# Loading q and k separately in another order, and a new instruction order, in a fused chunk-attention and token-mixing kernel

## Chip, core and metric

The kernel runs on one core of one Trainium2 chip. The metric is the device time of one execution in microseconds (us). The engines are TensorE (PE; its weight loads are listed apart as PEld), VectorE (DVE), ScalarE (ACT), GpSimd (POOL) and SyncE (SP). POOL and SP issue DMAs, each through its own queue; ACT can issue them too.

## What is computed

Inputs q, k, v are [8, 8, 576, 64] (batch, head, token, feature) in float32. Attention is within chunks of 64 tokens; its output, heads side by side, is the input x [8, 576, 512] of a mixing layer over the tokens:

```python
scores = scale * q_c @ k_c.T            # each chunk of 64 tokens, each head
attn   = exp(scores - max) / (sum + 1e-9)
x      = attn @ v_c                     # -> [B, S, 512]
wq, wk = x @ w_q, x @ w_k               # 512 -> 64
mixed  = (1/8 * wq @ wk.T) @ x          # over all 576 tokens of a batch
out    = relu(mixed) @ w_out            # float32 [8, 576, 512]
```

There is no softmax in the mixing, so the kernel computes `wq @ (wk.T @ x)`: G = wk.T x is a 64 x 512 matrix per batch.

## The kernel before

**Units.** The work is cut into 20 units, the list `pairs`. For each two batches there are five: two stretches of 256 tokens of the first batch, the last 64 tokens of both batches together (a "rest", units 2, 7, 12, 17), and two stretches of the second batch. Unit 19 is the last.

**Steps of a unit.** `turns` turns q and k with TensorE into PSUM (`tq`; two steps, q then k, in a whole unit, one in a rest) and evicts them to `qbd` (q in two halves) and `kt`. `attention` makes the scores (`S`, L407), the row maximum on DVE (`mx`, L420), the difference on DVE (`sub`, L431), exp on ACT (L441), turns the result (`E`, L453), evicts it (`et`), multiplies with v (`V`, L484; v carries a column of ones, which gives the sum), and then DVE adds 1e-9, takes the reciprocal and scales (`den`, `rec`, `x`). `project` turns x (`xT`, L536), evicts (`xt`), multiplies with the two small weights (`pj`, L553) and turns the wk part (`wkT`, `wkn`). `mixing` sums G over a batch (L607), evicts it (`g16`), multiplies with wq (`mix`, L647), applies relu on the way out (`rm`), multiplies with w_out (`out`, L696), evicts (`osb`) and stores. Evictions and casts can go to ACT or DVE; most of them stand under one helper, L308.

**The order.** Nothing is scheduled when the kernel is built. The string `ORDER` lists every step by its number with the engine behind it (p PE, a ACT, v DVE, s a store) and the PSUM banks that it takes; each engine runs its own steps in that order. An entry such as `i7.512` is a filler: a product of ones into bank 7, 512 columns wide, whose result is not used (L740). The string was made by a planner outside the kernel.

**The loads.** `LOADS` lists the loads in the order of GpSimd's queue: in the old kernel `q5` stands for q and k of unit 5, one DMA each (two each in a rest), `v5` for its v (two DMAs). Only q and k of unit 0 come by SP's queue, as float32 (`wide_in`), and are cast to f16 by ACT or DVE; the DMAs of GpSimd's queue cast on the way. `load_more` issues the list until it meets a v whose place in `v_all` is still held by an earlier unit; it goes on when that unit's V steps have been put in the order. The tiles of q and k lie in a pool of seven (`HOMES["qk"]`). The queue has eight completion semaphores, so that a load also waits for the landing of the eighth before it; the same holds for the stores.

**The stores.** A store is issued by SP. A tiny DMA (`held`, L268) that reads the last element of unit 4's v stands ahead of all stores in SP's queue.

Of the kernel before, what the change touches and what calls it, by code (L numbers as in the profile page):

```python
# [34 lines left out]


NQB, NG, NV = 3, 3, 8

HELD = 4
LATE = {("qk", 1, 0): 2.5, ("qk", 1, 1): 2.0}  # L40

HOMES = {
# [21 lines left out]
    "rm2": 3,  # L64
    "rm1": 2,
}
LOADS = "q1 v0 q2 v1 wqk v2 q3 q4 v3 q5 wo v4 q6 v5 q7 v6 q8 v7 q9 v8 q10 v9 q11 v10 q12 v11 q13 v12 q14 v13 q15 v14 q16 v15 q17 v16 q18 v17 q19 v18 v19"

ORDER = """
0a 1v i7.256 i6.256 i5.256 i7.256 i6.256 i5.256 i7.256 i6.256 i5.256 i7.256 i6.256 i5.256 i7.256 i6.256 i5.256
i7.256 i6.256 i5.512 i7.256 i6.256 7p0 3a 2a 9a 8v i7.512 i6.512 i5.512 i7.512 i6.512 i5.512 i7.512 i6.256
i5.256 10p1 11a i7.256 26p5 28a 4a 27a i7.256 12p0 29p4 13v 30a 14v 15a i7.512 i6.512 i3.512 i7.512 i6.256 31p4
32v i7.512 i6.512 i3.512 i7.256 53p0 55v 33v i7.512 i6.256 16p1 54a 56a 17a 34a i7.512 i6.512 i3.512 i7.512
i6.256 18p0 22p6 i5.256 57p4 i3.512 35p5 36a 23v 19v 20v 58v 24v 59v 21v 37p2 41p4 38v 60a 39v 42v 25v 61p0
88p1 62a 63p6 89a 90a 45p0 40v 64v 43v 65v 44v 91p2 66v i3.256 47p1 92a 67p3 93p6 107p2 i5.512 110p4 109a 108a
68a 46a 48v 6v 94v 5v 95v 111v i3.256 69p5 49p3 70v 71p2 72v 112p4 113v 96a 50a 97p6 51p7 98a 52v 153p3 156p6
73p7.2 103p0 154a 155a 157a 75a 74a 114v 99p4 104v 105v 100v 101v 106v 102v 115a 158p2 76p6 159v 77a 78p0 116p4  # L80
126p5 79a 117v 160v 118p6 122p0 84p4 172p2 175p3 123v 124v 119v 125v 173v 174v 120v 85v 121v 161a 127a 162p5
176a 163a 177p2 168p4 164p0 128p6 129a 199p6 130p7 178v 165v 166v 179v 169v 167v 82p2 131v 170v 200a 202a 201a
180a 203p6 132p7 204v 83a 171v 181p3 234p2 133a 182a 134p7.0 183p4 237p3 236a 136a 235a 135v 205v 184v 185v
186v 238a 137p0 239p2 139p6 206a 138a 207p4 86p5 208a 140a 253p4 240v 241v 256p0 209p6 187p2 255a 254a 242a
143p1 191p4 192a 257v 188v 189v 190v 210v 211v 258p2 212v 259v 145p0 146a 260v 193p4 243p6 194a 244a 87a 87s
299p0 302p4 249p6 245p2 300a 301a 144v 213p5 214a 195p1 196a 261a 250v 251v 246v 303v 252v 247v 248v 215p0
304p4 80p6 149p2 216a 217p7 197p0 150a 198a 305v 218v 318p1 306v 219p0.7 321p2 221v 322v 220a 319a 320a 222p4
272p7 223v 224p2 273a 323p0 262p7 324v 225a 263a 307a 147p4 226p5 345p7 325v 268p0 264p2 148a 148s 81v 81s 269v
265v 270v 266v 271v 227v 267v 308p4 230p6 346a 348a 347a 326a 309a 231a 349p7 380p0 310p4 314p2 383p6 350v 351v
315v 311v 312v 316v 382a 381a 352a 274p1 327p7 328a 151p0 275a 384v 385p6 313v 317v 386v 276p1 353p2 277a 152a  # L90
152s 354a 387v 228p3 229v 229s 337p1 278p0 338a 279a 333p4 329p6 334v 330v 335v 331v 332v 336v 399p2 280p3.0
402p1 355p6 282v 356v 357v 358v 401a 281a 400a 388a 232p3 339p0 340a 283p4 284v 359p2 285p6 341p0 403a 360a
342a 233a 233s 286v 404p4 361p2 389p1 343p0 295p6 362a 363p2 344a 364a 390a 296a 405v 406v 445p3 365p2.0 448p1
366v 367a 447a 395p6 449v 289p0 141p2 370p4 293p1 142a 142s 407a 294a 290a 396v 397v 398v 446v 371v 450p2 451v
408p6 368p4 297p7 409a 369a 298a 298s 467p6 464p0 466a 465a 452v 468v 414p2 410p4 391p6 392v 411v 415v 393v
394v 412v 416v 413v 417v 291p1 376p0 469p6 470v 374p4 453a 454p5 375a 471v 455a 420p2 418p4 421a 419a 377a
491p5 456p2 460p6 287p4 472a 493v 494v 457v 492v 461v 462v 463v 495p5 458v 496v 497v 459v 422p0 378p6 423a 288a
288s 424p0 473p7 425a 529p4 426p0.5 474v 498a 379a 379s 530a 475p6 428v 479p2 427a 476v 480v 526p4 292a 292s
477v 481v 478v 545p0 527a 528a 482v 429p6 499p1 430v 431p2 531p4 500a 432a 485p1 532v 548p6 501p2 502v 439p7
547a 549a 546a 503v 504v 533v 483p6 440a 484a 486a 534a 505p0 550p2 372p7 441p4 487p1 535p6 373a 373s 442a 551v  # L100
506v 552v 437p7 507p0 536a 553a 537p2 488v 508v 541p4 538v 509p6 489p0 542v 539v 554p1 510a 543v 540v 544v 490a
555a 511p0.6 560p2 556p4 561v 557v 562v 558v 559v 563v 438a 438s 512a 513a 564p7 516p0 435p6 514p4 566p2 443p3
515v 565a 517a 567a 568p2 433p7 569a 444a 444s 570p2 436a 434a 434s 571v 522p4 572p6.5 524p7 525a 574v 573v
# [6 lines left out]
def kernel(  # L110
# [10 lines left out]
    nc = tc.nc  # L121
# [120 lines left out]
    for e in LOADS.split():  # L242
        u = int(e[1:]) if e[1:].isdigit() else None
        rest = u is not None and pairs[u][1] is None
        if e == "wqk":
            landing("w", 1.7)
            loads.append((load_w, [], None))
        elif e == "wo":
            landing("wo", 3.3)
            loads.append((load_wo, [], None))  # L250
        elif e[0] == "q":
            for t in range(2):
                landing(("qk", u, t), 0.94 if rest else wide)
            loads.append((load_qk, [u], None))
        else:
            landing(("v", u), halves if rest else 2 * halves)
            loads.append((load_v, [u], next((w for w in heir_v if heir_v[w] == u), None)))


    made_v, held, opened = {None: 2}, [], []  # L260

    def load_more():
        while loads and made_v.get(loads[0][2], 0) == 2:
            load, args, _ = loads.pop(0)
            load(*args)

            if load is load_v and args == [HELD]:
                nc.sync.dma_start(const.tile([1, 2], F16, name="held")[:], v_all[0:1, slot[HELD] + 1, H - 1, D - 2 : D])  # L268
# [4 lines left out]
    def store(to, of):  # L273
        if opened:
            nc.sync.dma_start(to, of)
        else:
            held.append((to, of))

    load_more()

# [56 lines left out]
    def turns(u):  # L337
# [40 lines left out]
        for t in range(2):  # L378
            bk = Banks(1)

            def pe(t=t, bk=bk):
                tp = in_banks(bk, 512, F16)[:, 0].rearrange("p (j x r g) -> p j x r g", j=HP, x=4, r=R)
                for j in range(HP):
                    for r in range(R):
                        for o in range(2):
                            of = qk[u][:, t, 2 * j + o, r * D : r * D + D]
                            nc.tensor.transpose(tp[half(o), j, :, r, :], of, ident[:])  # L387

            n1 = add("tq", {"PE": 8 * 0.056}, pe, ready[t] if u == 0 else [landed(("qk", u, t))], form=TALL, takes=[bk], size=16)
            if u in heir:  # L390
# [4 lines left out]
    def attention(u, made):  # L395
# [73 lines left out]
        for fours in ([0], [1]) if m is not None else ([0, 1],):  # L469
# [6 lines left out]
            def pe_v(fours=fours, xp=xp):  # L476
# [14 lines left out]
                made_v[u] = made_v.get(u, 0) + 1  # L491
                load_more()

            den, rec = [], []

# [187 lines left out]
    def outs(u, at_tok, deps):  # L683
# [4 lines left out]
        for i in range(ni):  # L688

            wide = DM // 2 if (b, m, i) == (B - 1, NPB - 1, 1) else DM  # L690
            for at in range(0, DM, wide):
# [17 lines left out]
                def send(i=i, s=s):  # L709
                    t0 = 0 if m is None else 2 * P * m  # L710
                    if m is None:
                        for c in range(2):
                            store(out[b + c, S - C : S, :], osb[0][half(c), i, :])
                    elif turned(u, 1):
                        store(out[b, t0 + i * P : t0 + i * P + P, s], osb[0][:, i, s])
                    else:
                        rows = out[b, t0 : t0 + 2 * P, :].rearrange("(x p) d -> p x d", p=C)
                        for c in range(2):
                            store(rows[:, 1:3] if c else rows[:, 0:4:3], osb[0][half(c)])
# [14 lines left out]

    steps = [n for n in nodes if n.cost]
    for e in ORDER.split():
        what, eng, *at = re.split(r"([ipavs])", e, maxsplit=1)
# [5 lines left out]
        if eng == "s":  # L743
            n.send()
            continue
        for bk, i in zip(n.takes, at):
            bk.at = i
# [29 lines left out]
```

## Time and profile before

| what | value |
|---|---|
| median of 3 runs | 138.56 us (138.06 to 140.58) |
| the profiled execution's own time | 138.08 us |
| its span | 136.3 us, 4971 instructions |
| granted TensorE clock, mean | 0.995 |
| DMA traffic | 29.62 MB read from HBM, 9.44 MB written |
| fillers (L740) | 52, of them 30 of 256 and 22 of 512 columns |
| loads on GpSimd's queue | first issued at 1.43 us, last landing at 104.9 us |
| first store issued, last landing | 55.7 us, 134.97 us |

The span is what the profiler recorded of one execution; the time around it is some 1.8 us longer. A wait in the profile is put down to what came last by the trace. TensorE's matmuls overlap, and the ends that the profile shows are modelled, so that a full PE in a stretch does not say that nothing more fits in.

### The profile page before, as it was taken

The page shows a single profiled execution, that of the slowest core. Times are in us where ns is not written, and L with a number is a line of the kernel's source. Part 1 is how long each engine was busy: PE and PEld are TensorE (multiplying, and loading weights), DVE is VectorE, ACT ScalarE, POOL GpSimd, SP SyncE. Part 2 cuts the span into 40 slices and gives each one's busy share as a digit, 9 for nine tenths or more (in the row PEclk, how much of TensorE's full clock was granted, in tenths as well). Part 3 has the DMA queues.
Part 4 walks back from the last instruction along what each step waited for, and adds up shares of the span by engine and source line. Part 5 has one row for each costly group of instructions (what it writes and reads, how often), then busy time and mean ns, then how long its engine had stood idle before and what let it go on. Part 6 is the DMA issues. An engine that isn't in the chain of part 4 may idle for free.

```text
span 136.3 us, 4971 instructions
## 1 busy us (share of the span) xinstructions
PE 122.2 (90%) x2124; PEld 82.8 (61%) x2124; DVE 109.6 (80%) x210; ACT 100.0 (73%) x175; POOL 74.3 (55%) x96
## 2 busy tenths in 40 slices
PE   6999978897859999999999999999999998999910
PEld 4566556575546667776676867566677766544500
DVE  5429898899899799999999999989989998535220
ACT  6186674789738997969996878795888998568500
POOL 7969998745789896469992642679410000000000
PEclk9999999999999999999999999999999999999997
DMA  3999999999999999999999999999999614628883
GB/s 83 273 169 155 131 171 170 182 190 175 156 156 170 172 176 170 166 236 153 173 207 292 175 279 185 241 207 220 200 164 300 227 37 121 154 64 206 280 248 124
DMA packets 86249, 25.08 MB, mean 184 GB/s; under 512 B 78932, under 2 KB 81748, under 8 KB 86228
## 3 DMA queue, kind: packets, MB, share of 16 engines
q0 software_dynamic: 78752, 14.29, 130.1%
q1 hardware_dynamic: 7476, 10.49, 25.3%
q8 instruction: 16, 0.26, 0.7%
q14 instruction: 5, 0.04, 0.1%
HBM read 29.62 MB, written 9.44 MB: 287 GB/s over the span
## 4 chain that ended last, share of the span: by engine, by line
PE 61%; DVE 20%; ACT 10%; issue 3%; DVEq 1%; ACTq 0%
PE ps L696 21%; PE ps L387 7%; DVE mx L420 6%; PE ps L740 5%; DVE sh L431 5%; PE ps L536 5%; PE ps L484 5%; PE ps L647 4%; PE ps L407 4%; PE ps L453 4%; PE ps L553 3%; ACT es L441 3%; PE ps L607 2%; DVE xs L512 2%; ACT rm L669 2%
## 5 line engine op out<-in xcount | busy, mean ns | idle before, releaser
L696 PE MATMUL ps<-wo,rm 128*128 128x512 f16 (+1 forms) x148 | 35.7, 374 | 0.0
L229 POOL DMA_DIRECT2D v_all<-in_v_dram x33 | 29.0, 896 | 11.5 <-DMA qk<-in_k_dram 4.4
L512 DVE TENSOR_TENSOR xs<-ps,rec 128x512 f16<-128x512 f32 x36 | 23.9, 684 | 0.4
L420 DVE TENSOR_REDUCE mx<-ps 128x16 f32<-128x1024 f32 (+1 forms) x20 | 22.2, 1110 | 1.5 <-PE ps L407 1.3
L441 ACT ACTIVATE es<-sh 128x1024 f16<-128x1024 f32 (+1 forms) x20 | 19.5, 975 | 2.7 <-DVE sh L431 2.5
L308 ACT COPY qbd<-ps 64x512 f32<-64x512 f32 (+1 forms) x33 | 18.1, 548 | 4.1 <-PE ps L387 2.4
L387 PE MATMUL ps<-ident,qk 128*64 128x128 f16 x512 | 19.6, 221 | 1.2 <-DMA qk<-in_k_dram 1.0
L696 PEld LDWEIGHTS <-rm 128*128 128x128 f16 x148 | 13.2, 98 | 12.2 <-issue 0.2
L308 ACT COPY osb<-ps 128x512 f32<-128x512 f32 (+1 forms) x28 | 15.8, 586 | 6.5 <-PE ps L696 6.4
L431 DVE TENSOR_TENSOR sh<-ps,mx 128x1024 f32<-128x1024 f32 x16 | 19.5, 1221 | 0.4
L387 PEld LDWEIGHTS <-qk 128*64 128x64 f16 x512 | 15.7, 109 | 4.7 <-issue 1.5
L215 POOL DMA_DIRECT2D qk<-in_k_dram x15 | 13.5, 902 | 3.4 <-DMA v_all<-in_v_dram 1.7
L215 POOL DMA_DIRECT2D qk<-in_q_dram x15 | 13.8, 918 | 1.8 <-DMA qk<-in_k_dram 1.4
L669 ACT ACTIVATE rm<-ps 128x1024 f16<-128x1024 f32 (+1 forms) x13 | 14.1, 1098 | 0.5 <-PE ps L569 0.3
L407 PEld LDWEIGHTS <-qbd 128*128 128x128 f16 x288 | 10.7, 98 | 4.5 <-DVE qbd L308 1.2
L740 PE MATMUL ps<-ones 128*128 128x256 f16 (+1 forms) x52 | 12.2, 372 | 1.2 <-DVE ones L157 1.2
L407 PE MATMUL ps<-kt,qbd 128*128 128x64 f16 x288 | 11.9, 193 | 1.1 <-DVE qbd L308 0.5
L308 ACT COPY xt<-ps 128x512 f32<-128x512 f32 (+1 forms) x18 | 9.6, 554 | 3.3 <-PE ps L536 3.0
L484 PE MATMUL ps<-v_all,et 64*64 64x65 f16 x576 | 9.8, 195 | 2.3 <-ACT et L308 0.7
L453 PE MATMUL ps<-ident,es 128*128 128x128 f16 x144 | 11.4, 220 | 0.2 <-DVE den L498 0.2
L308 ACT COPY et<-ps 128x512 f32<-128x512 f32 (+1 forms) x18 | 9.7, 541 | 2.0 <-PE ps L453 1.9
L536 PE MATMUL ps<-ident,xs 128*128 128x128 f16 x144 | 11.0, 220 | 0.1
(57 smaller groups left out, 172.5 us busy)
## 6 DMA issues: line engine op xcount, KB each, us to landing
out_dram<-osb SPq DMA_DIRECT2D x31, 256.0 KB, 5.2
v_all<-in_v_dram POOLq DMA_DIRECT2D x31, 128.0 KB, 7.7
qk<-in_q_dram POOLq DMA_DIRECT2D x15, 256.0 KB, 7.4
qk<-in_k_dram POOLq DMA_DIRECT2D x15, 256.0 KB, 8.0
out_dram<-osb SPq DMA_DIRECT2D x10, 128.0 KB, 2.8
v_all<-in_v_dram POOLq DMA_DIRECT2D x10, 64.0 KB, 6.3
osb<-in_q_dram SPq DMA_DIRECT2D x1, 512.0 KB, 4.2
osb<-in_k_dram SPq DMA_DIRECT2D x1, 512.0 KB, 5.5
```

Source lines behind the costliest of these rows:

```text
L215: nc.gpsimd.dma_start(qk[u][:, t], rows)
L229: nc.gpsimd.dma_start(v_all[on, slot[u] + i, :, 0:D], v[b, :, of, :].rearrange("h p d -> p h d"))
L308: (nc.vector.tensor_copy if eng == "DVE" else nc.scalar.copy)(to, of)
L387: nc.tensor.transpose(tp[half(o), j, :, r, :], of, ident[:])
L407: nc.tensor.matmul(sp[:, i, j, c ^ turned(u, i), :], lhsT=st["qb", u][:, j, x].rearrange("p o s -> p (o s)"), rhs=st["kt", u][:, j, x * C ...
L420: nc.vector.tensor_reduce(mx[:], scores(), axis=AX.X, op=ALU.max)
L431: nc.vector.tensor_tensor(out=sh[:].rearrange("p x (g r) -> p x r g", r=R), in0=in_banks(bs, 512).rearrange("p i (x r g) -> p (i x) r g", ...
L441: nc.scalar.activation(es[:].rearrange("p x s -> p (x s)"), st["sh", u][:].rearrange("p x s -> p (x s)"), AF.Exp, scale=scale_attn,)
L512: nc.vector.tensor_tensor(out=to, in0=xp()[:, :, :, 0:D], in1=by, op=ALU.mult)
L536: nc.tensor.transpose(tx[:, f, i, :], xs[u][:, i, 2 * f : 2 * f + 2, :], ident[:])
L696: nc.tensor.matmul(in_banks(bo, wide)[:, 0], lhsT=st["rm", key][:, f, at_tok + i * P : at_tok + i * P + P], rhs=wo[:, f, s], start=(f == 0 ...
L740: nc.tensor.matmul(ps[:, at[0], 0 : at[1]], lhsT=ones[:, 0:P], rhs=ones[:, 0 : at[1]], start=True, stop=True)
```

## The change

`LOADS` has entries `Q5` and `K5` of their own, and another sequence. `load_qk` takes the parts that it is to load and makes the tile at the first of them. A load of q or k, like one of v, is now issued when both steps that read its place's former holder have been put in the order. The tiny DMA ahead of the stores and the list of held stores are gone. A store names its queue: `s` is SP's, `t` ScalarE's. `ORDER` is another one over the same steps, with 48 fillers; one store has the `t`.

```diff
-LOADS = "q1 v0 q2 v1 wqk v2 q3 q4 v3 q5 wo v4 q6 v5 q7 v6 q8 v7 q9 v8 q10 v9 q11 v10 q12 v11 q13 ...
+LOADS = "Q1 K1 Q3 K3 Q2 K2 v0 Q4 K4 v1 v2 Q5 K5 wqk v3 Q6 K6 v4 Q7 K7 wo v5 Q8 v6 K8 Q9 v7 K9 Q10 K10 Q11 Q12 K11 K12 v8 Q13 K13 v9 v10 v11 ...
 ORDER = """
-0a 1v i7.256 i6.256 i5.256 ...
-i7.256 i6.256 i5.512 i7.256 i6.256 7p0 3a 2a 9a 8v i7.512 i6.512 i5.512 i7.512 i6.512 i5.512 i7.512 i6.256
-i5.256 10p1 11a i7.256 26p5 28a 4a 27a i7.256 12p0 29p4 13v 30a 14v 15a ...
+1v 0a i7.256 i6.256 i5.256 ...
+i7.256 i6.256 i5.512 i7.256 i6.256 7p0 8v 3a 2v 6a 9a i7.512 i6.512 i5.512 i7.512 i6.512 i5.512 i7.256 10p1 11a
+i7.512 i6.512 i5.512 i7.256 12p0 26p7 13v 29p6 88p5 14v 28a 27a 30a i4.512 i3.512 i2.512 i4.512 91p7 15a i6.256
+31p0 92v 32v 89a ...
 ...
-523v 523s 577p2 575p0 578a 518p7 520p6 576v 519a 521a 521s 589p0 581p7 583p6 585p2 579p3 590a 584a 584s 586a
-586s 587p2 591p6 580v 592v 588v 582a 582s 592s 588s
+523a 523s 578a 520p0 576v 518p1 521v 581p6 583p0 519a 519s 584a 584s 579p1 580v 582a 582s 589p2 587p0 585p6
+590a 591p1 586a 592v 588a 588s 592s 586t
 """
-    def load_qk(u):
+    def load_qk(u, ts=(0, 1)):
         b, m = pairs[u]
-        if m is None:
+        if u in qk:
+            pass
+        elif m is None:
             qk[u] = const.tile([P, 2, H, D], F16, name=f"qk{u}")
 ...
-        for t, x in enumerate((q, k)):
+        for t in ts:
+            x = (q, k)[t]
 ...
-    def load_more():
-        while loads and made_v.get(loads[0][2], 0) == 2:
+    def load_more(key=None):
+        if key is not None:
+            made_of[key] = made_of.get(key, 0) + 1
+        while loads and (loads[0][2][1] is None or made_of.get(loads[0][2], 0) == 2):
             load, args, _ = loads.pop(0)
             load(*args)
-
-            if load is load_v and args == [HELD]:
-                nc.sync.dma_start(const.tile([1, 2], F16, name="held")[:], v_all[0:1, slot[HELD] + 1, H - 1, D - 2 : D])
-                opened.append(True)
-                for to, of in held:
-                    nc.sync.dma_start(to, of)
 ...
-            store(out[b, t0 + i * P : t0 + i * P + P, s], osb[0][:, i, s])
+            by.dma_start(out[b, t0 + i * P : t0 + i * P + P, s], osb[0][:, i, s])
 ...
-            n.send()
+            n.send(nc.sync if eng == "s" else nc.scalar)
```

In the last two rows of `ORDER`, 588 and 586 are the two half-width evictions of unit 19's last 128 tokens, 584 the full one before them, 580 and 582 those of unit 18, 592 that of the last rest; 589 and 590 are the last rest's mix and rm, 591 its out.

More of the change, by code (lines that the diff above doesn't have):

```diff
@@ L66 @@
 }
-LOADS = "q1 v0 q2 v1 wqk v2 q3 q4 v3 q5 wo v4 q6 v5 q7 v6 q8 v7 q9 v8 q10 v9 q11 v10 q12 v11 q13 v12 q14 v13 q15 v14 q16 v15 q17 v16 q18 v17 q19 v18 v19"
+LOADS = "Q1 K1 Q3 K3 Q2 K2 v0 Q4 K4 v1 v2 Q5 K5 wqk v3 Q6 K6 v4 Q7 K7 wo v5 Q8 v6 K8 Q9 v7 K9 Q10 K10 Q11 Q12 K11 K12 v8 Q13 K13 v9 v10 v11 Q14 K14 v12 Q15 K15 Q16 v13 K16 v14 Q17 K17 v15 Q18 v16 K18 v17 Q19 K19 v18 v19 "
 ORDER = """
-0a 1v i7.256 i6.256 i5.256 i7.256 i6.256 i5.256 i7.256 i6.256 i5.256 i7.256 i6.256 i5.256 i7.256 i6.256 i5.256
@@ new lines @@
+78p4 161a 123v 119v 124v 125v 120v 76p2 77a 121v 126p0 199p1 79v 177p6 200a 128p2 127a 178v 162p3 202a 129a
+163a 201a 130p2 179v 131a 180a 203p3 84p1 204v 82p2 205v 85a 168p6 206a 132p3 181p1 169v 83v 164p4 170v 182a
+234p2 165v 133v 166v 171v 134p3.1 236a 167v 235a 183p6 136a 187p4 135a 191p2 188v 184v 189v 207p3 190v 185v
+139p0 137p4 140a 192v 186v 138v 237p2 253p6 208a 238a 209p0 255a 193p7 210v 239p4 211v 194a 212v 256p2 254a
+240v 213p7 195p6 214a 257v 149p0 241v 215p7 145p2 216a 196a 217p7 150v 242a 258p4 218v 302p6 259v 299p7 303a
@@ new lines @@
+318p3 300a 146v 86p6 301a 260v 320a 197p2 304p0 198a 243p7 319a 305v 87a 87s 244a 143p2 345p3 306v 219p6.4 348a
+144a 321p7 347v 221a 220a 249p0 245p4 261a 346v 246v 250v 80p6 251v 247v 248v 322a 349p3 81a 81s 323p4 222p6
+350v 223a 252v 262p2 351v 224p0 263a 324v 147p3 225a 272p6 325v 380p2 273a 383p7 352a 382v 268p4 264p0 265v
+151p6 381a 266v 269v 270v 267v 384a 230p2 326a 271v 385p0 274p7 353p4 231v 307a 386v 327p2 275a 308p5 328a
+276p7 354v 309a 387v 148a 148s 314p4 277a 226p2 315v 316v 152a 152s 317v 278p7 310p0 279a 333p4 227a 311v 399p6
@@ new lines @@
+334v 312v 335v 313v 280p7.3 402p2 336v 281v 329p0 403a 355p4 330v 228p7 337p2 401a 331v 356v 332v 357v 282a
+338a 400a 358v 339p3 283p0 285p4 340v 284v 359p2 286a 341p6 232p3 360v 388a 342v 295p4 404p0 296a 343p6 361p2
+405v 141p4 344a 362a 363p2 448p6 142a 142s 364v 406v 365p2.5 229a 229s 464p4 449a 233v 233s 445p7 367a 366a
+407a 389p5 447v 368p2 446v 370p0 390a 369v 289p6 371a 408p5 466v 395p2 409a 391p0 376p7 392v 465a 396v 393v
+397v 394v 450p4 398v 377a 290a 467p0 451v 410p2 468a 414p6 374p1 411v 412v 452v 297p0 375a 418p1 453a 413v
@@ new lines @@
+469p4 415v 416v 293p2 419a 417v 470v 454p1 491p3 420p6 471v 298a 298s 455a 291p7 421a 294a 493v 460p4 456p0
+472a 492v 422p2 457v 458v 494v 459v 495p3 423a 287p6 461v 462v 496v 424p2 473p0 425a 497v 378p1 474a 463v 498a
+475p2 288v 288s 479p4 379a 379s 526p0 480v 292a 292s 481v 426p1.6 482v 529p7 476v 427a 428v 527a 477v 429p4
+478v 530a 483p6 430v 528a 431p2 499p7 432a 531p0 484v 545p4 532v 548p5 500a 546a 501p6 485p2 549a 502v 533v
+439p3 547a 486a 550p4 503v 504v 534a 372p2 551v 441p6 535p0 505p1 373a 373s 442a 552v 487p2 506a 536a 507p1
@@ L106 @@
+488a 508v 537p4 541p6 553a 538v 542v 509p2 489p1 437p0 490v 539v 543v 440a 540v 554p1 510a 544v 511p2.3 555a
+438a 438s 556p6 560p4 512v 513a 561v 564p1 557v 558v 562v 516p2 565a 435p0 559v 563v 517a 514p6 566p1 515v
+433p2 567a 568p1 443p3 569a 434a 570p1 524p6 444a 444s 571v 436a 436s 572p1.7 522p0 574v 573a 525v 577p2 575p6
+523a 523s 578a 520p0 576v 518p1 521v 581p6 583p0 519a 519s 584a 584s 579p1 580v 582a 582s 589p2 587p0 585p6
+590a 591p1 586a 592v 588a 588s 592s 586t
 """
@@ L246 @@
             landing("w", 1.7)
-            loads.append((load_w, [], None))
+            loads.append((load_w, [], ("w", None)))
         elif e == "wo":
             landing("wo", 3.3)
-            loads.append((load_wo, [], None))
-        elif e[0] == "q":
-            for t in range(2):
+            loads.append((load_wo, [], ("w", None)))
+        elif e[0] in "qQK":
+            ts = {"q": (0, 1), "Q": (0,), "K": (1,)}[e[0]]
+            for t in ts:
                 landing(("qk", u, t), 0.94 if rest else wide)
-            loads.append((load_qk, [u], None))
+            loads.append((load_qk, [u, ts], ("qk", next((w for w in heir if heir[w] == u), None))))
         else:
             landing(("v", u), halves if rest else 2 * halves)
-            loads.append((load_v, [u], next((w for w in heir_v if heir_v[w] == u), None)))
-    made_v, held, opened = {None: 2}, [], []
-    def load_more():
-        while loads and made_v.get(loads[0][2], 0) == 2:
+            loads.append((load_v, [u], ("v", next((w for w in heir_v if heir_v[w] == u), None))))
+    made_of = {}
+    def load_more(key=None):
+        if key is not None:
+            made_of[key] = made_of.get(key, 0) + 1
+        while loads and (loads[0][2][1] is None or made_of.get(loads[0][2], 0) == 2):
             load, args, _ = loads.pop(0)
             load(*args)
-            if load is load_v and args == [HELD]:
-                nc.sync.dma_start(const.tile([1, 2], F16, name="held")[:], v_all[0:1, slot[HELD] + 1, H - 1, D - 2 : D])
-                opened.append(True)
-                for to, of in held:
-                    nc.sync.dma_start(to, of)
[L273 to L277, printed above, removed]
     load_more()
@@ L712, in send @@
                         for c in range(2):
-                            store(out[b + c, S - C : S, :], osb[0][half(c), i, :])
+                            by.dma_start(out[b + c, S - C : S, :], osb[0][half(c), i, :])
                     elif turned(u, 1):
-                        store(out[b, t0 + i * P : t0 + i * P + P, s], osb[0][:, i, s])
+                        by.dma_start(out[b, t0 + i * P : t0 + i * P + P, s], osb[0][:, i, s])
                     else:
@@ L718, in send @@
                         for c in range(2):
-                            store(rows[:, 1:3] if c else rows[:, 0:4:3], osb[0][half(c)])
+                            by.dma_start(rows[:, 1:3] if c else rows[:, 0:4:3], osb[0][half(c)])
                 n1 = add("out", {"PE": wide / 512 * 0.864}, pe_o, deps + [landed("wo")], form=FULL, takes=[bo], size=4)
@@ L736 @@
     for e in ORDER.split():
-        what, eng, *at = re.split(r"([ipavs])", e, maxsplit=1)
+        what, eng, *at = re.split(r"([ipavst])", e, maxsplit=1)
         at = [int(x) for part in at for x in part.split(".") if x]
```

44 lines of the change are left out of this document (10 added, 34 removed).

## The prediction

> **What bounds the kernel now.** I read the busy shares first, then the busy time by stretch, then who waited for whom, then the landing of each load and the end. By the shares no engine is full:
>
> ```profile
> ## 1 busy us (share of the span) xinstructions
> PE 122.2 (90%) x2124; PEld 82.8 (61%) x2124; DVE 109.6 (80%) x210; ACT 100.0 (73%) x175; POOL 74.3 (55%) x96
> ```
>
> The stretches tell more. After the length stand the busy times of PE, PE's weight loads, DVE, ACT and POOL, then the granted clock, the DMA share and GB/s. The first stretch begins with unit 0's max on DVE (10.2), the second with unit 3's.
>
> ```profile
> 10.20:22.95 12.75, 11.76 (x251) 8.35 (x247) 11.68 (x25) 7.90 (x14) 12.70 (x16) 1.00 2.00 157
> 22.95:50.00 27.05, 22.63 (x457) 15.82 (x451) 24.69 (x45) 21.61 (x35) 20.52 (x26) 1.00 1.99 171
> 50.00:80.00 30.00, 29.45 (x579) 21.36 (x574) 28.99 (x58) 25.65 (x48) 20.88 (x26) 1.00 1.89 199
> 80.00:110.00 30.00, 29.70 (x550) 20.53 (x549) 28.35 (x52) 24.65 (x47) 11.98 (x15) 1.00 1.63 216
> 110.00:130.00 20.00, 19.65 (x208) 10.85 (x206) 11.10 (x24) 14.23 (x27) 0.00 (x0) 1.00 0.58 155
> 130.00:136.30 6.30, 0.00 (x0) 0.00 (x0) 1.02 (x2) 0.00 (x0) 0.00 (x0) 0.89 0.59 175
> ```
>
> From 10.2 to 110 DVE is busy 93.7 of 99.8 us, and its longer waits are few:
>
> ```profile
> DVE mx L420 <- PE ps L407: 1.3, 2, 1.0
> DVE den L498 <- PE ps L484: 1.0, 2, 0.5
> DVE g L308 <- PE ps L607: 1.0, 2, 0.7
> DVE wkr L308 <- ACT es L441: 0.4, 1, 0.4
> DVE rec L502 <- DVE den L498: 0.3, 1, 0.3
> DVE rm L667 <- PE ps L647: 0.3, 1, 0.3
> ```
>
> So DVE sets the pace there, with PE close behind from 50 us on. After 110 PE does: the chain of waits lies on it without a break from 113.66 (batch 6's G) to 130.0. The last 6.3 us are evictions, stores and the closing. The profiled execution took 138.08 us around its span of 136.3, 0.5 under the median 138.56; I sum against 138.08.
>
> **The loads.** GpSimd's queue carries them in the order of LOADS. Once the stream runs, a 256 KB q or k lands some 1.45 us after the one before it, a v (two DMAs) takes 1.7, a rest's q or k 0.83 (spacings of landings in this trace). One k, issued at 2.44, by its own answer (KB, us to landing):
>
> ```profile
> qk<-in_k_dram POOLq DMA_DIRECT2D x1, 256.0 KB, 7.2
> ```
>
> so K1 lands at 9.6; K3 at 19.9, K4 at 24.3, K5 at 28.5, K6 at 35.7, and PE takes each up within 0.6 us. v0 lands at 11.3 and is used at 15.5. Thus q and k come just in time and v early: the change trades one for the other. Yet no DVE wait above is ended by a load, and DVE loses little by them.
>
> **The change, term by term.**
>
> *Start, -0.35.* K0's two casts are split over DVE (0.43) and ACT (0.62); before, ACT did both (6.77 to 7.91). The fillers between unit 0's turns go from nine (6.16 to 8.06) to seven, some 1.5 us, so the k turn starts near 7.75, not 8.00. Behind it stand 0.64 of turn and 0.75 of fillers: S0 near 9.1 (9.47 before), max 0 near 9.85 (10.21). Bounds: 0 (an eviction of the same qbd tile waits) and -0.6 (the fillers alone decide).
>
> *Ahead of max 1, +1.0.* PE now has unit 3's turns before S1, and DVE has unit 3's k eviction before max 1. K3 is the fourth load: 9.6 and twice 1.45, 12.5. Its turn ends at 13.2, the eviction (0.68) runs to 13.9, max 1 starts near 14.0, against 12.61. DVE ended unit 0's subtract near 12.3, so it idles about 0.9 and a little more. Behind the waiting turn PE holds S1, so nothing else for DVE can come. Bounds: 0.3 (K3 as close as v0's halves were, 0.85 apart) and 2.2 (spacing of K4 after Q4, 2.66).
>
> *v0 behind six loads, +0.2.* Q2 and K2 add 1.66 (14.2 to 14.7), v0 1.7: 15.9 to 16.6. Unit 0's turned weights are evicted near 16.5, so V0 starts near 16.7 and DVE, done with unit 1's subtract and a rest eviction at 16.95, waits 0.1 to 0.2. v1 lands at 20.4 to 21.4 for a use near 21. By the same sums K5 comes at 24.1 to 25.7 and K6 near 30 (earlier), wqk at 25 to 27 for a use after max 4 near 27, wo near 37.5 (31.1 before) for a use near 41; from K8 on the two streams agree. I walked DVE's list on from here: max 3 starts near 20.8 with 11.4 us of DVE work done, where before it is 22.95 with 13.9. Before, 11.4 us were done by about 20.4; these 0.4 and the extra cast's 0.43, which is in the new count alone, are the +0.85 of the three terms so far. Bounds of this one: 0 and 3 (second rival).
>
> *DVE's work, +0.65.* Up to max 19 (108.79) the order gives DVE more: one cast 0.43 (in idle time, not counted), one whole rm 1.30, two xt 1.38, one rest xt 0.41, one rest et 0.41, three rest evictions 1.26, one wt 0.68; less three whole evictions 2.04, two et 1.36, two g16 0.84, two clears 0.54. Net +1.09, or +0.65 without the cast. DVE is the pace, so it shows in full; if all of it fell into DVE's waits it would be 0. ACT, 24.65 busy of 30 from 80 on, takes the reverse.
>
> *The other waits of DVE, 0.* 2.9 us of them over 0.15 us lie between 22.95 and 109 (sum of the gaps in the trace). The new order has its own, which no row shows: -2.9 if all go, as much more if they double; nearest to the rows is no change.
>
> *PE's tail, +0.25.* From batch 6's G on, both orders hold the same PE steps; only the last rest's mix (0.23) moves from the wait for rm 19 to behind three outs. From max 19 to V19 (108.79 to 114.33) the path stays near 5.5: DVE loses one xt (0.41) between max and subtract, ACT gains some 0.4 of evictions ahead of unit 19's exp. Four fewer fillers (23 of 256 and 25 of 512 columns for 30 and 22) are -0.1 within waits: nothing.
>
> *Stores.* The tiny load-dependent DMA goes:
>
> ```profile
> SPq L268 <- DMA v_all<-in_v_dram: 31.0, 1, 31.0
> ```
>
> It ends at 33.6; the first store is ready at 55.7, so 0. At the end:
>
> ```profile
> 130.03 1.02 DVE L308 COPY osb<-ps 128x512 f32<-128x512 f32 x2 [0.55 <-PE ps L696]
> ...
> 130.89 2.29 SPq L275 DMA_DIRECT2D out_dram<-osb  x3
> ...
> out_dram<-osb SPq DMA_DIRECT2D x1, 128.0 KB, 2.3
> ```
>
> The last piece is ready at 131.05 but issued at 132.64, behind two others, and lands at 134.97, 5.0 after PE's end. In the new order unit 18's pair is sent sooner, DVE has one last eviction (0.69) instead of two, SP issues its two stores 0.8 and 1.45 after PE's end, and ACT, with nothing behind it, issues the other beside them. With 2.3 to 2.8 to landing that is 4.0 after PE's end: **-1.0**; bounds 0 (landing 3.2, as the store at 130.89, with the issues slower) and -1.6 (the whole wait of the last piece). The Trainium skill ("DMA: Bandwidth & Descriptors", section "Issuing engines are not separate DMA queues") says that a second issuing engine saves only the sequencer's time, usually small beside the DMA. By it alone this term would be near 0 and the sum 139.8; the row's 1.6 us between ready and issued is sequencer time, and not small here.
>
> **Sum:** -0.35 + 1.0 + 0.2 + 0.65 + 0.25 - 1.0 = +0.75: 138.8 us, a change of 0.5%. About 2% (2.8 us) is what a measurement of this kernel tells from no change.
>
> **Rivals.**
> 1. *Loads stop pacing, faster.* With q and k ahead of need, all 2.9 us of later DVE waits and the 1.0 ahead of max 1 go: 134.9. For it: K3 to K6 land within 0.6 us of use. Against: DVE is full in those stretches already.
> 2. *A late v holds PE's queue, slower.* V0 stands ahead of S2 and S3, V1 ahead of unit 5's turns; DVE drains meanwhile. If the stream runs as between K3 and K4 (4.4 us for two loads, not 2.9), v0 comes near 18.1 and v1 near 22.6: some 1.5 us each, 141.8. It exceeds 2% once both together lose 2 us more than summed. For it: that spacing is in the trace. Against: most spacings there are 1.45. The Trainium skill's rule (same page, "Rules for kernel authors": issue a DMA early, wait on it late) speaks for this rival.
> 3. *The second queue brings nothing*: both last stores share the DMA engines and land as late: 139.8.
>
> **Chances.** Forecast 0.45, rival 1 0.17, rival 2 0.26, rival 3 0.12. Faster by over 2% 0.17, within 0.57, slower 0.26. The range reaches toward both outer cases, 135.2 to 141.6; the forecast's own is 137.0 to 140.7 (its bounds on the early waits and DVE's work).
>
> **What would show it.** Max 0 near 9.85; max 1 near 14, after a DVE wait that ends with unit 3's k turn; K3 landing at 12.5, v0 near 16; max 19 at 110 to 110.5; PE's end 21.4 after it; the last landing 4.0 after PE's end, with one store on ACT's queue. Wrong if DVE's waits after 23 us differ from 2.9 by over 2 us, or if a V step waits over 1 us for its load.

## The result

Over 20 runs of each, the changed kernel takes 137.86 us in the median and the kernel before 138.47: a ratio of 0.9944, 95% interval 0.9923 to 0.9965. That is 0.6 us faster: within the 2% that the prediction called no change, but on the other side of zero from the forecast sum of +0.75. The profiled execution of the changed kernel took 137.94 us around a span of 136.14. Before's profiled execution (138.08) lies 0.4 under its own median, so the two profiles differ by 0.14 us only; the runs of single parts below carry the verdicts. Three ratios below (the kernel without the tiny DMA, and the two with a reordered tail) come out low, because 5 of the 17 runs of the kernel before beside them took 140.0 to 140.3 us; with the other twelve they are about 0.996, 0.993 and 0.993.

The busy shares of the changed kernel:

```profile
## 1 busy us (share of the span) xinstructions
PE 121.7 (89%) x2120; PEld 82.6 (61%) x2120; DVE 109.3 (80%) x210; ACT 100.5 (74%) x175; POOL 74.5 (55%) x96
```

DVE has as many instructions as before and 0.3 us less to do, ACT 0.5 more. The stretches of the changed kernel, with the columns as in the prediction and the first cuts at its own starts of max 0 and max 3:

```profile
9.70:20.67 10.97, 9.28 (x196) 6.49 (x192) 9.43 (x16) 6.86 (x12) 8.82 (x11) 1.00 2.14 167
20.67:50.00 29.33, 26.15 (x568) 19.08 (x566) 27.34 (x57) 24.75 (x45) 24.84 (x32) 1.00 1.99 173
50.00:80.00 30.00, 29.73 (x559) 21.11 (x558) 28.20 (x54) 25.43 (x44) 20.45 (x25) 1.00 1.93 202
80.00:110.00 30.00, 28.48 (x528) 19.88 (x525) 28.09 (x52) 23.89 (x43) 12.41 (x15) 1.00 1.56 204
110.00:130.00 20.00, 19.64 (x206) 10.62 (x203) 11.39 (x25) 14.43 (x27) 0.00 (x0) 1.00 0.58 158
130.00:136.10 6.10, 0.00 (x0) 0.00 (x0) 0.51 (x1) 0.00 (x0) 0.00 (x0) 0.88 0.63 176
```

DVE remains the fullest engine up to 80 us, and after 110 PE is, as before. Unit 3's max starts at 20.67 instead of 22.95, with less work of DVE done by then. What DVE waited for between 9 and 110 us in the changed kernel (total, times, longest):

```profile
DVE mx L413 <- PE ps L400: 3.0, 2, 2.3
DVE den L490 <- PE ps L477: 2.0, 4, 0.9
DVE kt L300 <- PE ps L379: 1.3, 1, 1.3
```

The 2.3 of the first line stand before max 0. The third line is new and is the wait that the prediction put ahead of max 1. DVE's timeline there (start, us, instruction, idle time before and what ended it):

```profile
9.70 1.22 DVE L413 TENSOR_REDUCE mx<-ps 128x16 f32<-128x1024 f32 x1 [2.31 <-PE ps L400]
...
13.52 0.69 DVE L300 COPY kt<-ps 128x512 f32<-128x512 f32 x1 [1.34 <-PE ps L379]
14.13 1.23 DVE L413 TENSOR_REDUCE mx<-ps 128x16 f32<-128x1024 f32 x1
...
20.67 1.22 DVE L413 TENSOR_REDUCE mx<-ps 128x16 f32<-128x1024 f32 x1
```

DVE idles 1.34 us until unit 3's k has been turned (K3 landed at 12.7), max 1 starts at 14.13 and max 3 at 20.67; the forecast had 12.5, 14.0 and 20.8. In the eight profiles with this order and these loads (unit 1's scores behind unit 3's k turn) that wait is 0.8 to 2.4 us long and K3 lands at 12.0 to 13.5, so that one profile tells the size only roughly.

The end of the changed kernel, where PE's last product ends at 129.79 (evictions, and the issues of stores on SP's and ACT's queues):

```profile
128.66 1.26 SPq L711 DMA_DIRECT2D out_dram<-osb  x2
...
129.36 0.38 ACTq L707 DMA_DIRECT2D out_dram<-osb  x1
129.82 0.69 DVE L300 COPY osb<-ps 128x512 f32<-128x512 f32 x1 [1.22 <-PE ps L688]
130.01 1.03 SPq L707 DMA_DIRECT2D out_dram<-osb  x1
131.14 2.01 SPq L705 DMA_DIRECT2D out_dram<-osb  x2
```

SP's last three issues take 1.03, 1.37 and 0.59 us (the last two are the x2 row), so the last store is issued 2.8 us after PE's end, not 1.45, and lands at 134.92, 5.14 after it. The forecast had 4.0, before had 4.98.

Cut at the same events, the two profiled executions differ as follows (us):

| stretch | before | changed | difference | forecast |
|---|---|---|---|---|
| to max 0 | 10.21 | 9.70 | -0.51 | -0.35 |
| max 0 to max 19 | 98.58 | 99.11 | +0.53 | +1.85 |
| max 19 to PE's end | 21.20 | 20.97 | -0.23 | +0.25 |
| PE's end to the last landing | 4.98 | 5.14 | +0.16 | -1.0 |
| last landing to the span's end | 1.34 | 1.22 | -0.12 | 0 |
| outside the span | 1.77 | 1.80 | +0.03 | 0 |

Two terms are off by over 1 us, with opposite signs. The miss of the second stretch is in DVE's own steps, and part of the gain in the medians came from a term that the prediction had priced at nothing, the tiny DMA.

### The profile page after: what moved, and what is told of

Same layout as the page of the kernel before. It is cut to its first block, busy times and chain, and to the rows that moved or that the text cites. A ratio compares the mean times of both kernels' runs of the same rounds, so it can differ in the third digit from the quotient of the medians.

```text
span 136.1 us, 4949 instructions
## 1 busy us (share of the span) xinstructions
PE 121.7 (89%) x2120; PEld 82.6 (61%) x2120; DVE 109.3 (80%) x210; ACT 100.5 (74%) x175; POOL 74.5 (55%) x96
## 3 DMA queue, kind: packets, MB, share of 16 engines
HBM read 29.62 MB, written 9.44 MB: 287 GB/s over the span
## 4 chain that ended last, share of the span: by engine, by line
PE 60%; DVE 13%; ACT 10%; DMA 6%; issue 5%; POOL 2%; POOLq 0%; DVEq 0%; ACTq 0%
PE ps L688 22%; PE ps L379 7%; DMA qk<-in_q_dram 6%; PE ps L528 5%; PE ps L477 5%; PE ps L400 4%; PE ps L545 4%; PE ps L639 4%; DVE xs L504 4%; PE ps L446 3%; ACT es L434 2%; DVE mx L413 2%; PE ps L599 2%; PE ps L732 2%; ACT et L300 1%
## 5 line engine op out<-in xcount | busy, mean ns | idle before, releaser
L300 ACT COPY osb<-ps 128x512 f32<-128x512 f32 (+1 forms) x28 | 15.3, 574 | 4.6 <-PE ps L688 4.0
L300 ACT COPY qbd<-ps 64x512 f32<-64x512 f32 (+1 forms) x28 | 15.7, 565 | 2.9 <-PE ps L379 1.7
L216 POOL DMA_DIRECT2D qk<-in_k_dram x15 | 13.5, 902 | 3.6 <-DMA qk<-in_k_dram 2.7
L300 ACT COPY et<-ps 128x512 f32<-128x512 f32 (+1 forms) x19 | 10.4, 550 | 5.5 <-PE ps L446 5.3
L732 PE MATMUL ps<-ones 128*128 128x512 f16 (+1 forms) x48 | 11.9, 383 | 1.2 <-DVE ones L155 1.2
L477 PE MATMUL ps<-v_all,et 64*64 64x65 f16 x576 | 10.4, 195 | 1.8 <-DVE xs L504 1.1
L477 PEld LDWEIGHTS <-et 64*64 64x64 f16 x576 | 7.8, 107 | 6.6 <-issue 2.6
```

The lines of the kernel that those rows point to most:

```text
L300: (nc.vector.tensor_copy if eng == "DVE" else nc.scalar.copy)(to, of)
L477: nc.tensor.matmul(to[half(k ^ i), i if ni == 2 else w, x, :], lhsT=et[half(k), i, h // 2, h % 2, :], rhs=v_all[half(k), slot[u] + i, h, 0:W],
```

## The experiments

Each kernel was measured beside the kernel before on the same chip (median 138.5 to 138.6 each time); ratios are to it.

### Does the second queue bring anything?

*The changed kernel with its last store on SP.*

```diff
-590a 591p1 586a 592v 588a 588s 592s 586t
+590a 591p1 586a 592v 588a 588s 592s 586s
```

> The changed kernel with its last store on SyncE's queue instead of ScalarE's; all else as changed (137.86). If the second queue is worth what the prediction summed (issue time saved), the store is issued some 0.6 after the last rest's two, at 133.15 in the changed kernel's trace, and lands 0.5 to 1.0 later: 138.4 to 138.9. If the stores of the end share the DMA engines and only their bytes count: 137.9.

Measured: 137.26 us, ratio 0.9916 (0.9886 to 0.9947). Its end (issues on SP; PE's last product ends at 129.23):

```profile
129.46 0.61 SPq L707 DMA_DIRECT2D out_dram<-osb  x1
130.16 1.27 SPq L705 DMA_DIRECT2D out_dram<-osb  x2
131.48 0.58 SPq L707 DMA_DIRECT2D out_dram<-osb  x1
```

Four issues on one queue take about 0.6 us each and the last lands 4.93 after PE's end, 0.2 sooner than with ACT's help. ACT's store in the changed kernel took 4.1 us to land, SP's last four here 2.7 to 3.5. The time is below both that were expected, though its interval overlaps that of the changed kernel.

*The kernel before with its last store on ACT's queue* (and the few lines that let a store name its queue).

```diff
-586s 587p2 591p6 580v 592v 588v 582a 582s 592s 588s
+586s 587p2 591p6 580v 592v 588v 582a 582s 592s 588t
```

> The kernel before with its last store on ScalarE's queue, nothing else changed. If issue time sets the end: the last piece goes out at 131.1 instead of 132.64 and the last landing comes 0.5 to 0.9 sooner: 137.6 to 138.0 against 138.5. If bytes set it: 138.5, and the last landing stays within 0.2 of 134.97.

Measured: 138.51, ratio 1.0011 (0.9993 to 1.0028). ACT's store is issued at 131.68 and lands 4.1 later; SP's next issue takes 1.21.

*The tail reordered so that the last rest's work ends early, all stores on SP.*

```diff
-523a 523s 578a 520p0 576v 518p1 521v 581p6 583p0 519a 519s 584a 584s 579p1 580v 582a 582s 589p2 587p0 585p6
-590a 591p1 586a 592v 588a 588s 592s 586t
+523a 523s 578a 520p0 576v 518p1 589p2 521v 519a 519s 581p6 590a 583p0 584a 584s 579p1 580v 591p3 582a 582s
+587p0 592v 592s 585p6 588a 588s 586v 586s
```

> The changed kernel with all stores on SyncE and another order of the last steps: the last rest's mix stands before unit 18's and 19's output steps, its output before unit 19's two half-width ones, and its two stores before the last two. TensorE then ends with a half-width step, after which one eviction of 0.4 and one store of 128 KB remain. If the end is a chain of eviction, issue and landing: the last landing 3.8 to 4.2 after TensorE's end instead of 4.9, TensorE's end 0.2 sooner, 136.2 to 136.6 against 137.3 of the same kernel with the old tail. If the bytes of the last stores set the end: 137.0 to 137.3.

Measured: 137.55, ratio 0.9876 (0.9811 to 0.9941); last landing 4.75 after PE's end. That is above both expected times, and the landing is 0.2 sooner than with the old tail, not 0.7 to 1.1.

*The same with the last store on ACT's queue (586t).*

> The same kernel as the one with the new tail, with the very last store on ScalarE's queue. If the second queue saves the issue time of the store ahead of it: 0.3 to 0.6 under the one with all stores on SyncE. If a store on the second queue lands later and slows SyncE's next issues, as the traces of the changed kernel and of the one before with a ScalarE store look: 0 to 0.5 over it.

Measured: 137.57, ratio 0.9894 (0.9834 to 0.9954); last landing 5.21 after PE's end. In none of the three pairs did the store on ACT's queue gain time: what rival 3 said of the queue held, though not its time of 139.8. In each the last landing comes 0.2 to 0.5 later with it, but of the five kernels further down that keep it four (old loads, and the three with added work) land 4.75 to 4.91 after PE's end and one (unit 1's scores first) 5.05, so that this difference is not firm.

### Loads and order apart

*New loads, old order:* the changed kernel with before's `ORDER`.

```diff
-1v 0a i7.256 i6.256 i5.256 ...
+0a 1v i7.256 i6.256 i5.256 ...
```

> The old instruction order with the new load order (no held store, all stores on SyncE). If the load order is a gain by itself, because q and k come earlier: about 137.9. My theory is that it only serves the new instruction order: the old one uses v0 at 15.5, v1 at 18.0 and v2 at 19.5, which the new load order lands at 16.6, 21.4 and 22.5, so that the early part loses 2 to 3 us: 140.5 to 141.5.

Measured: 142.88, ratio 1.0314 (1.0282 to 1.0346). What DVE waited for between 9 and 110 us:

```profile
DVE den L490 <- PE ps L477: 3.7, 4, 2.2
DVE mx L413 <- PE ps L400: 1.6, 2, 1.3
DVE xt L300 <- PE ps L528: 1.2, 1, 1.2
```

The time is 1.4 above the expected range. The v that now comes late holds `den` of unit 1 for 2.2 us, and what stands behind it: max 3 starts at 27.3. This is the mechanism of rival 2, shown in an order that takes v early.

*Old loads, new order:* the changed kernel with before's `LOADS`.

```diff
-LOADS = "Q1 K1 Q3 K3 Q2 K2 v0 Q4 K4 v1 v2 Q5 K5 wqk v3 Q6 K6 v4 ...
+LOADS = "q1 v0 q2 v1 wqk v2 q3 q4 v3 q5 wo v4 ...
```

> The new instruction order with the old load order. If loads are hidden anyway: 137.9. My theory: unit 1's scores stand behind unit 3's k turn on TensorE, and the old load order lands k of unit 3 at 19.9 instead of 12.7, with nothing else to do for VectorE: max 1 starts near 21 instead of 14.1, and most of the 7 us stays to the end: 142 to 145.

Measured: 145.95, ratio 1.0546 (1.0495 to 1.0597). What DVE waited for:

```profile
DVE kt L300 <- PE ps L379: 9.9, 1, 9.9
```

K3 is behind nine loads, and DVE stands still for 9.9 us ahead of max 1. So either part alone loses 4.4 or 7.4 us; the two belong together.

*The new order with unit 1's scores ahead of unit 3's k turn,* so that DVE need not wait for K3.

```diff
-... i4.512 91p7 15a i6.256
-31p0 92v 32v 89a ...
+... i4.512 31p2 91p7 15a i6.256
+32v 92v 89a ...
```

> The changed kernel with unit 1's scores ahead of unit 3's k turn on TensorE, and unit 1's max ahead of unit 3's k eviction on VectorE (PSUM banks 0, 1 and 2, 3 change names from there on, so that the scores find free banks). It takes away the 1.3 us in which VectorE waits for K3. If each us that VectorE is kept busy early comes out at the end: 136.5. If the wait only moves on to v0, which lands at 16.6 and holds V0: max 1 near 12.7 instead of 14.1, but a new wait before the sums of unit 0, max 3 at most 0.4 sooner than 20.7, and 137.5 to 137.9.

Measured: 137.95, ratio 0.9934 (0.9894 to 0.9974). Max 1 starts at 13.5 instead of 14.1 (3.3 us after max 0 instead of 4.4), but DVE waits 1.1 us at 16.4 instead, and max 3 starts at 21.5. On PE, ahead of that wait, stands this:

```profile
15.36 0.38 PE L733 MATMUL ps<-ones 128*128 128x512 f16 x1 [0.70 <-DVE kt L301]
```

The filler `i7.512` waits until DVE has evicted unit 3's k from bank 7, which now comes behind max 1, and the rest's turn, for whose eviction DVE then waits, stands behind that filler. The new wait is thus made by the edit itself and not by a load (v0 landed at 16.46, Q2 and K2 by 14.53). Whether the 1.3 us could be won with that filler elsewhere isn't shown.

### Whose microseconds count

In three places of the changed kernel (ahead of max 9, max 13 and max 16, or of the next product with w_out) work without use was added: two fills of 128x512 float32 on DVE (485 ns each), two products on ACT (626 ns each), or four fillers of 512 columns on PE. Measured from the end of the instruction ahead of them to the start of the one behind, they take 3.6 us in all on DVE (each second fill waits 0.17 for the first) and 3.3 on ACT, where they overlap their neighbours; on PE it is 2.6.

```diff
+            nc.vector.memset(spare[:], 0.0)                     # first kernel, six times
+            nc.scalar.mul(spare[:].rearrange(...), some[:, 0:4], 0.0)   # second kernel, six times
+i6.512 i6.512 i6.512 i6.512 86p6                                # third kernel, in three places
```

> The changed kernel with six extra fills of a spare tile on VectorE, two ahead of the max of units 9, 13 and 16, some 2.9 us in all. If VectorE paces the middle, as the prediction took it: 139.9 to 140.8. If it has slack there and another engine paces: at most 138.6.

> The changed kernel with six extra products on a spare tile on ScalarE at the same three places, some 3.2 us in all. ScalarE is busy 8 of 10 us there: if it has slack, 137.9 to 138.9; if each of its us holds the evictions that TensorE waits for: 140 to 141.

> The changed kernel with twelve extra fillers of 512 columns on TensorE, four ahead of an output step after the max of units 9, 13 and 16, some 2.6 us in all. If VectorE alone paces the middle and TensorE has slack: at most 138.5. If TensorE is as full as the page's tenths say: 140.0 to 140.5. With both close, about half: 139.2.

Measured: 140.30 (ratio 1.0101, 1.0043 to 1.0160) with more work on DVE, 140.42 (1.0121, 1.0051 to 1.0191) on ACT, 139.11 (1.0030, 0.9988 to 1.0072) on PE. Against 137.86 that is 0.7, 0.8 and 0.5 us of time for each us of work; by the intervals each is known to some 0.3 only (an estimate). ACT, 24 busy of 30 us, is about as dear here as DVE, 28 of 30.

### The tiny DMA

*The kernel before without it.* The stores then wait for nothing.

```diff
-HELD = 4
+HELD = None
...
-    made_v, held, opened = {None: 2}, [], []
+    made_v, held, opened = {None: 2}, [], [True]
```

> The kernel before without the tiny DMA that reads unit 4's v ahead of the stores; nothing else. The first store is ready 22 us after that DMA ends, so 138.5, the same as before, by every theory but one: if stores that are held back had spared the loads, it would differ by more than 0.4.

Measured: 137.96, ratio 0.9919 (0.9880 to 0.9958). By the medians (137.96 against 138.53) this one edit gains 0.6 us, as much as the whole change. Its profile differs in the first two loads. Size and time to landing, before:

```profile
osb<-in_q_dram SPq DMA_DIRECT2D x1, 512.0 KB, 4.2
osb<-in_k_dram SPq DMA_DIRECT2D x1, 512.0 KB, 5.5
```

and without the tiny DMA:

```profile
osb<-in_q_dram SPq DMA_DIRECT2D x1, 512.0 KB, 4.0
osb<-in_k_dram SPq DMA_DIRECT2D x1, 512.0 KB, 5.0
```

The tiny DMA is issued 31 us later and can't slow these loads. But its target is a tile of its own (4 bytes, taken as 32 with rounding) in the pool `const`; the pool `work` with all `osb` and most qk tiles is taken to lie behind it, so that they are shifted by 32 bytes. No trace shows addresses; the offsets below are counted from the place without the tile. Six kernels separate the DMA from the place; their edits are the line of the DMA (in the last row of the table the tile alone is put into the changed kernel with all stores on SP):

```diff
-  nc.sync.dma_start(const.tile([1, 2], F16, name="held")[:], v_all[...])
+  nc.sync.dma_start(const.tile([1, 32], F16, name="held")[:, 0:2], v_all[...])   # 64 bytes; 64, 128, 256 columns: 128, 256, 512
+  nc.vector.memset(const.tile([1, 2], F16, name="held")[:], 0.0)                 # the tile alone, no DMA
```

> The kernel before with its tiny DMA kept, its tile 64 bytes instead of 4, so that all later tiles of SBUF lie 64 bytes beyond where they lie without the tile (before: 32). Theory (the 32-byte shift slows the transfers; in the profiled runs unit 0's k landed 1.83 us after its q with the shift, 1.46 to 1.51 without): 138.0 us as without the tiny DMA, k 1.5 us after q. Rival (the tiny DMA or the wait on SP's queue costs by itself): 138.5, whatever the spacing.

> The kernel before without its tiny DMA, but with a tile of 4 bytes in its place, cleared by DVE at the start: the 32-byte shift stays, the DMA and its wait go. Theory (the shift): 138.5 us, unit 0's k 1.83 us after its q. Rival (the tiny DMA): 138.0, k 1.5 us after q or not.

> The changed kernel with all stores on SP's queue and a tile of 4 bytes at the place where the tiny DMA's stood, cleared by DVE: only the 32-byte shift is new against the changed kernel with all stores on SP (137.26). Theory (the shift costs 0.5 us there too): 137.7 to 137.9 us, k 1.83 us after q. Rival: 137.3, as without the tile.

> The kernel before with its tiny DMA kept, its tile 512 bytes, so that the later tiles lie as without it modulo 512. Alignment theory: unit 0's k lands 1.5 us after its q and the time is 138.0 us, as without the tiny DMA. Rival (the tiny DMA and its wait cost by themselves): 138.5.

> As the kernel with the tile of 512 bytes, with 256: the later tiles lie 256 bytes beyond. Alignment theory with 256 bytes as the limit: k 1.5 us after q, 138.0 us; with 512 as the limit: 1.83 and 138.5. Rival (the tiny DMA): 138.5 with either spacing.

> As the kernel with the tile of 512 bytes, with 128. Alignment theory with 128 as the limit: k 1.5 us after q, 138.0 us; with a coarser limit: 1.83 and 138.5 (64 bytes gave 1.86 and 138.54). Rival (the tiny DMA): 138.5 with either spacing.

| kernel | tiny DMA | tile's bytes | k lands after q, us | last landing after PE's end | median, us | ratio (95%) |
|---|---|---|---|---|---|---|
| before | yes | 32 | 1.84 | 4.98 | 138.5 | 1 |
| tile alone | no | 32 | 1.83 | 5.01 | 138.44 | 1.0004 (0.9979 to 1.0030) |
| 64 bytes | yes | 64 | 1.86 | 4.99 | 138.54 | 0.9993 (0.9970 to 1.0017) |
| 128 bytes | yes | 128 | 1.85 | 4.86 | 138.56 | 0.9993 (0.9970 to 1.0015) |
| 256 bytes | yes | 256 | 1.50 | 4.78 | 138.12 | 0.9957 (0.9930 to 0.9983) |
| 512 bytes | yes | 512 | 1.49 | 4.81 | 138.48 | 0.9974 (0.9950 to 0.9998) |
| no tiny DMA | no | 0 | 1.50 | 4.81 | 137.96 | 0.9919 (0.9880 to 0.9958) |
| changed, all on SP | no | 0 | 1.51 | 4.93 | 137.26 | 0.9916 (0.9886 to 0.9947) |
| the same with the tile | no | 32 | 1.83 | 5.20 | 137.66 | 0.9944 (0.9913 to 0.9974) |

(The runs with 512 bytes fall into two groups, 137.65 to 137.77 and 138.41 to 138.80; the ratio says more of it than the median.) The loads of the tile alone, without any tiny DMA, are slow again:

```profile
osb<-in_q_dram SPq DMA_DIRECT2D x1, 512.0 KB, 4.1
osb<-in_k_dram SPq DMA_DIRECT2D x1, 512.0 KB, 5.5
```

and those with the tiny DMA and a tile of 256 bytes are fast:

```profile
osb<-in_q_dram SPq DMA_DIRECT2D x1, 512.0 KB, 3.9
osb<-in_k_dram SPq DMA_DIRECT2D x1, 512.0 KB, 4.9
```

The place decides the pace of these transfers: shifted by 32, 64 or 128 bytes the k lands 1.83 to 1.86 us after its q, by 0, 256 or 512 bytes (called aligned from here on) 1.49 to 1.51, with or without the tiny DMA. With time it goes the same way: every shifted version of before has an interval around 1, every aligned one lies below it. That is 0.3 to 0.6 us. In the changed order the place isn't firm in the time: 0.9916 without the tile and 0.9944 with it overlap. The expectation for 64 bytes had the limit too fine. How the shift reaches the end is seen in part: 0.2 us in the last landing (0.05 with 128 bytes). At the start q itself lands at 4.66 to 4.73 in the aligned versions of before and at 4.88 to 4.92 in the shifted ones of this table, but max 0 does not follow it in before's order (10.15 to 10.88 aligned, 10.20 to 10.43 shifted), where turns and fillers stand between. In the changed order it mostly does: max 0 starts 4.85 us after q's landing without the tile (9.44) and 4.91 with it (9.94); of the other profiles of that order two have 5.4 and 5.6. The rest of the 0.3 to 0.6 us isn't located.

The tiny DMA by itself leaves one trace: from the last landing to the span's end 1.33 to 1.34 us pass in the five kernels that keep it and have their last store on SP, 1.21 to 1.22 in the four without. Whether it costs more than that 0.12 can't be told from the ratios, about 0.996 without it and 0.9957 and 0.9974 with it.

The last row of the table also tells what the new loads and the new order bring by themselves, as it has before's place and stores on SP alone: 0.9944, which is 0.8 us less than before (0.4 to 1.2), while the old order without the tiny DMA at that place takes as long as before (1.0004). In its profile 0.27 us of the gain lie ahead of max 0, 0.49 between max 0 and max 19 and 0.22 from there to PE's end. On the aligned place the medians with and without new loads and order, 137.26 and 137.96, are 0.7 apart.

## Why the prediction was wrong

The prediction forecast 0.75 us lost, and the kernel gained 0.6. The step that failed most is the cost of new loads and new order together: they were to cost 1.75 us and gained 0.7 to 0.8, and by the count below most of that is the term for DVE's work. The tiny DMA was to bring nothing and its place brought 0.3 to 0.6. Against these the stores were to bring 1.0 and brought nothing. That the sum still came within 1 us of the measured time is luck: these errors have opposite signs. By term:

*Start, -0.35: right.* It came to -0.51; that q and k land 0.05 and 0.41 sooner was not in it.

*Ahead of max 1, +1.0, and v0 behind six loads, +0.2: right.* K3 12.7 (12.5), the wait 1.34, max 1 14.13 (14.0), v0 16.6 (15.9 to 16.6), max 3 20.67 (20.8). The sums from spacings of 1.45, 1.7 and 0.83 us held, and no V step waited over 1 us for its load. Part of the closeness is luck: in the other seven profiles with this order and these loads max 1 starts at 13.5 to 15.0 and max 3 at 20.8 to 21.8.

*The other waits of DVE, 0: right by its own test.* After 23 us DVE idles 3.7 us (gaps over 0.15) where before had 2.9; 0.9 of that is one wait of unit 15's `den` at 96.48, behind 1.3 us in which PE stands idle (up to 94.85) for nothing that the profile shows. The kernel with all stores on SP, which is the same up to there, waits 0.15 there and 2.6 in all. Rival 1 got nothing here, rival 2 neither.

*DVE's work, +0.65: wrong, the step with the largest error that can be counted.* Taken from one start to the next, without the idle time over 0.12 us, DVE's instructions between max 0 and max 19 occupy 94.96 us before and 93.89 in the changed kernel: -1.1 (94.8 to 95.1 in nine profiles with the old order, 93.6 to 93.9 in seven with the new one). Three things were mis-sized. The `rm` that moves to DVE was counted as a whole one, 1.30, and is a short one, 0.68: -0.62, and the sum of lengths is then 0. Lengths were added where the next instruction starts before the last one's end, as in these rows of the changed kernel, 0.68 long and 0.60 apart:

```profile
18.88 0.68 DVE L413 TENSOR_REDUCE mx<-ps 128x8 f32<-128x512 f32 x1
19.47 0.68 DVE L504 TENSOR_TENSOR xs<-ps,rec 128x512 f16<-128x512 f32 x1
20.07 0.68 DVE L420 TENSOR_TENSOR sh<-ps,mx 128x512 f32<-128x512 f32 x1
```

Counted so, the moved steps come to about -0.5 instead of 0. And steps that are in both orders occupy about 0.5 less in the new one, on average an `x` 613 ns instead of 628 and a `sub` 1171 instead of 1181, which no row of before could show. The prediction also let ACT take "the reverse" at no cost. ACT's busy time between max 0 and max 19 rose by 1.3 us, and the run with more work on ACT shows that such a microsecond costs some 0.8. So the exchange between the two engines could have brought little either way. What part of the -1.1 reached the time isn't isolated by a run, so that the cause of the 0.7 to 0.8 us is counted in the profiles and not shown.

*PE's tail, +0.25: wrong in sign, -0.23.* The last rest's mix does move behind the outs, but it took the same 0.23 of PE before: there was no wait for `rm` to hide it in. In unit 19 xT comes 0.1 us sooner after max 19, and the mix behind it another 0.1 sooner.

*Stores, -1.0: wrong.* The step that failed is "SP issues its two stores 0.8 and 1.45 after PE's end": they went out 1.4 and 2.8 after it, because the issue ahead of them took 1.03 us and the first of them 1.37. The last one then landed 2.4 later, as forecast. ACT's store took 4.1 us to land, not 2.3 to 2.8, but landed at 133.5, ahead of SP's last, and did not set the end. So issuing beside SP saved nothing: +0.16, and in no pair of runs did it save time. The rule of the Trainium skill that the prediction set against this term ("DMA: Bandwidth & Descriptors", section "Issuing engines are not separate DMA queues") was the better guide: the runs agree with it, with 1.0011 for the old kernel.

*The tiny DMA, "so 0": wrong, and part of the measured gain.* The argument that the DMA ends 22 us before the first store is ready was true and beside the point: with the DMA its tile goes, and with the tile the shift of what lies behind it. Without the DMA the kernel before takes 137.96, the changed kernel 137.86. That these two are so close does not say that loads and order bring nothing: with all stores on SP they bring 0.7 to 0.8, and the changed kernel's store on ACT's queue seems to give most of that back (137.86 against 137.26), though this last difference isn't firm.

Of the kernels tried, the changed one with all stores on SP's queue, at 137.26, has the lower median than both; its interval and that of the changed kernel (0.9886 to 0.9947 and 0.9923 to 0.9965) overlap.

## What to carry to other kernels

Before pricing a removed instruction at nothing, see what goes with it: its buffer, and so the place of every buffer behind it. Price a list of moved steps by the time from one start to the next, and charge the engine that receives them; an engine at 80% can be on the path as much as one at 94%. A searched load order and a searched instruction order that fit each other can cost 4.4 or 7.4 us if only one is taken, and gain under 1 together. When a change has several parts, give each a kernel that leaves out that part alone, the place of its buffers included, before one part is given the whole gain.

## What the runs showed of the hardware

A 512 KB load of float32 in pieces of 512 bytes (two tokens of 64 features) takes 1.83 to 1.86 us behind another one where its tile in SBUF is shifted by 32, 64 or 128 bytes, and 1.49 to 1.51 where it is shifted by 0, 256 or 512: 23% more, whatever the offset (the kernels of the table). The Trainium skill ("DMA: Bandwidth & Descriptors", section "How a descriptor splits into AXI transactions") says that a descriptor is cut into transactions that start at multiples of 256 bytes. By its count, and as an estimate, a piece of 512 bytes needs three transactions instead of two when it starts off such a multiple, and 17, 18 or 20 of its beats of 32 bytes instead of 16 for 32, 64 and 128 bytes. The measured step of 256 agrees with it, if the place without the tile is itself such a multiple, which no trace shows; that the cost is the same for all three offsets fits a count of transactions better than one of beats.

A store on ACT's queue among the last stores on SP's took 3.6 to 4.2 us from issue to landing in the eight kernels that have one, where the prediction had 2.3 to 2.8. Of SP's issues behind it one or two took 1.0 to 1.5 us instead of 0.6. They lengthened as well, to 0.94 and 1.08, in the changed kernel with the shifted tiles and all stores on SP, so that ACT's queue isn't the only reason.
